# First dense layer of two thirds of the units in seven block products on pairs of units, layers run in turn

## The chip, the cores and the metric

The kernel runs on one core of one Trainium2 chip. The metric is device time in microseconds of one execution, the median of the runs. A TensorE instruction multiplies a stationary block of up to 128x128 (loaded by a weight load of its own) with a moving block of up to 512 columns and adds into a PSUM bank; VectorE (DVE), ScalarE (ACT) and GpSimd (POOL) do elementwise work, and SyncE (SP) issues the transfers.

## The reference, cut to what matters

A chunked linear-attention layer feeds two dense layers. Only the dense part is changed in its arithmetic.

```python
# x (4,8,768,32), a (4,8,768), B and C (4,8,768,16); chunks in the original are 32 long
attn_out = _attn_ref(x, a, B, C)               # decayed C.B scores times x, plus a carried state
x = attn_out.transpose(0, 2, 1, 3).reshape(3072, 256)
def _moe_ref(x, w_in, w_out):                  # layer A; w_in (256,2048), w_out (2048,256)
    h = x @ w_in
    g = h * (1.0 / (1.0 + np.exp(-1.702 * h)))
    return g @ w_out
def _moe2_ref(x, w_in, w_out):                 # layer B, on the result of layer A
    h = x @ w_in
    g = h * np.clip(h + 3.0, 0.0, 6.0) / 6.0
    return g @ w_out
```

## The kernel before

**Tiles.** The 3072 tokens are cut into six blocks of 512 (numbered k), the 2048 hidden columns into sixteen of 128 (m). A unit is one layer, one k and one m: kind A for the first dense layer pair, kind B for the second, so 2 x 6 x 16 = 192 units. A unit first forms a 128x512 bank of hidden values from 256 input features (`l1`, L722), then passes it through its activation, then adds its share to two 128x512 output banks (`l2`, L756). Values and weights are each held as a top half in reduced precision and the rest (`wh`/`wl`, `gh`/`gl`), and three of the four cross products are computed: so `l1` is 2 feature halves x 3 = 6 matmuls of 512 columns and `l2` is 2 output halves x 3 = 6. In this text "first layer" of a unit is `l1`, "second layer" is `l2`; kinds A and B are the two networks.

**Activation.** Kind A: ACT applies the gelu in the bank (L739), casts the top half (L743), DVE or POOL subtracts to get the rest (L753). Kind B: ACT relu into `gg` (L741), DVE clips and multiplies (L748), ACT casts (L743), POOL subtracts (L753).

**Attention.** 32 pieces q (8 chunks of 96 tokens x 4 batches): DVE scans a decay matrix (L460, twice), PE forms scores (L535), DVE or ACT with POOL multiply (L538, L545), PE forms outputs (L556), ACT and DVE split them into the token block's input (L570, L574) and DVE turns the carried state (L583). Chunks 0 to 3 form scores in fp32 from 16 rows, four products at once on the array; chunks 4 to 7 from stacked bf16 parts that pass through DRAM (`stk_store`, `stk_load`).

**Weights** arrive packed in 32 loads and are decoded on the chip (L328 to L362): ACT scales and extracts (L334, L344), DVE joins (L350), ACT casts (L356), POOL subtracts (L362). All 32 stay resident.

**Order.** Nothing runs in loops: the function lists every operation with an engine, an estimated duration and a due time, and `Schedule.run` (L118) sorts them greedily by engine, dependences, free buffers and due times into one straight program. Each engine then runs its list strictly in that order and waits where a value is not there. `order` (L295) gives the units their due times: A0, A1, then B0 and A2 in alternation, B1, then A3, B2, A4, B3, A5, B4, B5. `PIECE` (L70) gives those of the attention pieces: after the first six, five ahead of A1, five ahead of A2, six ahead of A3 and the last ten during A3/B2 and A4/B3. The second layer of a unit is due two units after its first (`LAG`). The pools of buffers are fixed tiles; the hidden banks `h` are two.

Of the kernel before, what the change touches and what calls it, by code (L numbers as in the profile page):

```python
# [61 lines left out]


def YBANK(q):
    if q < 6:
        return f"{'ys'[q % 2]}:y{q}"
    return f"{'ys'[q % 2] if q < 16 else 'y'}:y{q}"


def PIECE(q, lead):  # L70

    if q < 6:
        return 6 + 2.2 * q + 3 * (q > 3)
    if q < 11:
        return lead["A", 1] - 20 + 4 * (q - 6)
    if q < 16:
        return lead["A", 2] - 30 + 5 * (q - 11)
    if q < 22:
        return lead["A", 3] - 42 + 7 * (q - 16)
    k, i = (3, q - 22) if q < 27 else (4, q - 27)  # L80
    return lead["A", k] + 2 + 8 * i
# [831 lines left out]
```

## Time and profile before

| | us |
|---|---|
| median of three runs | 592.24 (591.18 to 592.87) |
| span of the profiled execution (the page gives no other time of it) | 591.0 |
| TensorE matmuls busy, 3260 instructions | 580.1 |
| DVE busy, 453 instructions | 296.8 |
| ACT busy, 596 instructions | 316.3 |
| POOL busy, 165 instructions | 202.3 |

The busy time of PE in the page counts each matmul until its modelled end, so the ends of neighbours overlap; the distance from one to the next is read from the chain or the timeline. A group's mean hides its spread; the source view gives least, median and greatest. The chain of waits is followed back from the last instruction, so an engine with most of the chain sets the end.

### The profile page before, as it was taken

How to read it: one execution, taken by the hardware profiler on the slowest of the kernel's cores; microseconds unless marked ns; L12 is line 12 of the kernel's file. 1: busy time of each engine (PE TensorE's matmuls, PEld its weight loads, DVE VectorE, ACT ScalarE, POOL GpSimd, SP SyncE). 2: the span in 40 equal slices, each digit the busy share in tenths (PEclk: the TensorE clock that was granted, in tenths of full speed). 3: DMA queues.
4: the chain of work that ended last, by engine and by line, in shares of the span. 5: the costliest groups of instructions: out<-in, count | busy, mean ns of one | idle time of the engine just before them, and what ended most of it. 6: DMA issues, size and time to landing. Idle time of an engine off the chain costs nothing.

```text
span 591.0 us, 8575 instructions
## 1 busy us (share of the span) xinstructions
PE 580.1 (98%) x3260; PEld 466.6 (79%) x3260; DVE 296.8 (50%) x453; ACT 316.3 (54%) x596; POOL 202.3 (34%) x165
## 2 busy tenths in 40 slices
PE   8799999999999999999999999999999999999997
PEld 6587777778888887778778888778888888888885
DVE  6899996745434647777533454642322222322221
ACT  2788746677776455454444545334544544444443
POOL 2747200224544445461001662000544000454542
PEclk9899999999999999999999999999999999999999
DMA  8856641522212939566240163200000100000101
GB/s 187 287 141 199 174 116 69 171 76 104 81 62 62 239 93 259 140 165 174 88 145 1 29 151 102 90 24 1 1 1 0 37 1 1 0 2 0 37 0 36
DMA packets 42776, 52.36 MB, mean 89 GB/s; under 512 B 22752, under 2 KB 34384, under 8 KB 42736
## 3 DMA queue, kind: packets, MB, share of 16 engines
q1 hardware_dynamic: 41888, 51.47, 30.7%
q10 hardware_dynamic: 848, 0.35, 0.3%
q8 instruction: 25, 0.41, 0.3%
q14 instruction: 15, 0.12, 0.1%
HBM read 41.21 MB, written 10.60 MB: 88 GB/s over the span
## 4 chain that ended last, share of the span: by engine, by line
PE 95%; DMA 2%; DVE 1%; ACT 1%; issue 0%; SPq 0%; ACTq 0%
PE h L728 45%; PE acc L774 45%; PE y L556 2%; DMA raws<-in_wu 1%; PE s L535 1%; DVE l L460 1%; DMA late<-in_bcz 1%; PE acc L535 1%; PE s L556 1%; PE acc L728 0%; DVE xs L583 0%; DVE xt L574 0%; DVE gl L753 0%; ACT raws L344 0%; ACT gg L787 0%
## 5 line engine op out<-in xcount | busy, mean ns | idle before, releaser
L753 POOL TENSOR_TENSOR gl<-gg,gh 128x512 fp32r<-128x512 f32 x95 | 127.1, 1340 | 274.8 <-ACT gh L743 256.5
L728 PE MATMUL h<-xt,wh 128*128 128x512 f32 x568 | 157.0, 399 | 1.5 <-DVE xt L574 0.8
L748 DVE SCALAR_TENSOR_TENSOR gg<-gg,h 128x512 f32<-128x512 f32 x96 | 65.8, 685 | 135.9 <-ACT gg L741 135.8
L728 PEld LDWEIGHTS h<-xt,wh 128*128 128x128 f32 x568 | 105.6, 190 | 26.0 <-issue 2.1
L753 DVE TENSOR_TENSOR gl<-h,gh 128x512 fp32r<-128x512 f32 x94 | 64.8, 689 | 108.1 <-ACT gh L743 104.9
L774 PE MATMUL acc<-gh,wh 128*128 128x512 f32 x288 | 112.4, 390 | 0.0
L739 ACT ACTIVATE h<-h 128x512 f32<-128x512 f32 x94 | 54.7, 582 | 106.0 <-PE h L728 105.8
L774 PE MATMUL acc<-gh,wl 128*128 128x512 f32 x276 | 109.1, 395 | 0.0
L741 ACT ACTIVATE gg<-h 128x512 f32<-128x512 f32 x96 | 57.4, 598 | 82.4 <-PE h L728 77.3
L774 PE MATMUL acc<-gl,wh 128*128 128x512 f32 x288 | 89.8, 389 | 0.0
L743 ACT CAST gh<-gg 128x512 fp32r<-128x512 f32 x96 | 59.6, 621 | 50.1 <-DVE gg L748 50.1
L728 PE MATMUL h<-xt,wl 128*128 128x512 f32 x272 | 84.8, 393 | 0.0
L460 DVE TENSOR_TENSOR_SCAN l<-l,pat_sb 112x448 f32<-112x448 f32 x52 | 63.3, 1229 | 3.2 <-DMA l<-acl_d 3.1
L774 PEld LDWEIGHTS acc<-gl,wh 128*128 128x128 f32 x288 | 54.1, 188 | 11.5
L774 PEld LDWEIGHTS acc<-gh,wh 128*128 128x128 f32 x288 | 54.1, 188 | 10.9
L774 PEld LDWEIGHTS acc<-gh,wl 128*128 128x128 f32 x276 | 51.8, 188 | 11.9 <-issue 1.2
L728 PEld LDWEIGHTS h<-xt,wl 128*128 128x128 f32 x272 | 51.4, 190 | 11.3 <-issue 0.2
L362 POOL TENSOR_TENSOR wl<-dec,wh 128x512 fp32r<-128x512 f32 x23 | 33.6, 1466 | 71.3 <-ACT wh L356 68.9
L743 ACT CAST gh<-h 128x512 fp32r<-128x512 f32 x94 | 55.2, 587 | 3.6
L728 PE MATMUL h<-xt,w_early 128*128 128x512 f32 x192 | 51.9, 392 | 0.0
L774 PE MATMUL acc<-gh,w_late 128*128 128x512 f32 x108 | 42.4, 392 | 0.0
L728 PEld LDWEIGHTS h<-xt,w_early 128*128 128x128 f32 x192 | 35.6, 188 | 7.6 <-issue 0.3
(96 smaller groups left out, 561.7 us busy)
## 6 DMA issues: line engine op xcount, KB each, us to landing
l<-acl_d SPq DMA_DIRECT2D x26, 392.0 KB, 4.9
raws<-in_wu SPq DMA_DIRECT2D x18, 512.0 KB, 4.8
st<-scr SPq DMA_DIRECT2D x8, 896.0 KB, 6.0
scr<-tsplit SPq DMA_DIRECT2D x32, 168.0 KB, 2.8
raw<-in_wu SPq DMA_DIRECT2D x10, 512.0 KB, 4.0
xs<-in_xs SPq DMA_DIRECT2D x8, 384.0 KB, 5.9
early<-in_wu SPq DMA_DIRECT2D x4, 512.0 KB, 8.4
scr<-tsplit SPq DMA_DIRECT2D x16, 112.0 KB, 2.7
```

Of the source, the lines that this page charges most:

```text
L362: e.tensor_tensor(out=w_lo[p], in0=B_(f"dec:{p}").bitcast(F32), in1=w_hi[p].bitcast(F32), op=ALU.subtract)
L460: nc.vector.tensor_tensor_scan(t, a, m, 0.0, ALU.mult, ALU.add)
L535: nc.tensor.matmul(out=ps[:, k, :], lhsT=l, rhs=r, start=True, stop=True)
L556: nc.tensor.matmul(out=yv[32 * k:32 * k + 32, g, :], lhsT=x[0:E, b, h * D:(h + 1) * D], rhs=B_(f"gm:{q}.{g}")[:, k, :], start=True, stop=True)
L728: nc.tensor.matmul(out=ps, lhsT=w[p][:, 128 * j:128 * j + 128], rhs=x[:, xp, j, a:b], start=not lo and (xp, j) == (1, 0), stop=lo and j == 1)
L739: nc.scalar.activation(ps, ps, AF.Gelu_apprx_sigmoid)
L741: nc.scalar.activation(B_(f"gg:{u}")[:, 0:n], ps, AF.Relu, bias=3.0)
L743: nc.scalar.copy(B_(f"gh:{u}")[:, 0:n], ps if kind == "A" else B_(f"gg:{u}")[:, 0:n])
L748: nc.vector.scalar_tensor_tensor(out=g, in0=g, scalar=6.0, in1=B_(hn(u))[:, 0:n], op0=ALU.min, op1=ALU.mult)
L753: e.tensor_tensor(out=B_(f"gl:{u}")[:, 0:n], in0=g, in1=B_(f"gh:{u}")[:, 0:n].bitcast(F32), op=ALU.subtract)
L774: nc.tensor.matmul(out=acc[d], lhsT=w[p][:, 256 + 128 * d:384 + 128 * d], rhs=g, start=(m == 0 and a == 0 and d not in seen), stop=(m == N ...
```

## The change

**Seven products.** The 64 units of kind A on token blocks 0 to 3 stay as they are. The other 128 (kind A on blocks 4 and 5, kind B on all six) are worked in groups of four: a pair of unit columns m times a pair of token blocks, so 1024 tokens. A group's first layer is a 2x2 by 2x2 product of blocks (two unit columns x two feature halves, two feature halves x two token blocks). Eight block products of 3 matmuls become seven, in Winograd's form: four sums S of weight blocks (`s_comb`) and four of input blocks T1 to T4 (`operands`) are formed and split into halves, and the products go into three banks V, Ra and Rb, with DVE additions (`p_add`) between that carry partial results over through `pu` tiles: u2 = Ra + p1, u3 = Ra + p1, hs = Rb + u3, and two in the bank. A group is called a quad here, and there are 32. Second layers stay 6 matmuls a unit.

**Layers in turn.** The order becomes A0, A1, A2, A3 (units), A4+5 (8 quads), B0+1, B2+3, B4+5 (8 quads each). All 32 attention pieces come ahead of A4+5. All of them form scores in fp32 from 16 rows, two pieces in one go; the bf16 stacks and their DRAM passes are gone. Kind B weights are decoded from A4+5 on, into the sixteen buffers that kind A frees.

**Buffers.** One pool `bx` of 21 tiles of 4 KB holds raw weights, inputs, split inputs, block sums and results by turn; attention's tiles (`ov1` to `ov4`) are reopened for the quads' partial results. Half of the subtractions of A1 to A3 go from DVE to POOL (`GLP`).

```diff
-    for m in range(NM):
-        order += [whole("A", 0, LEAD + m)] * (LEAD + m < NM) + [whole("A", 1, m)]
-    for m in range(NM):
-        order += [whole("B", 0, m), whole("A", 2, m)]
-    order += [whole("B", 1, m) for m in range(NM)]
-    for k in range(3, NK):
-        order += [whole("A", k, m) for m in range(NM)] + [whole("B", k - 1, m) for m in range(NM)]
...
+    units = [("A", k, m) for k in range(STD) for m in range(NM)]
+    sups = [("A", k) for k in range(STD, NB6, 2)] + [("B", k) for k in range(0, NB6, 2)]
...
+PK = (48, 4, 88, 5, 114, 7, 156, 5)
...
+def PIECE(q):
...
     if q < 11:
-        return lead["A", 1] - 20 + 4 * (q - 6)
+        return PK[0] + PK[1] * (q - 6)
...
+    return PK[6] + PK[7] * (q - 22)
...
+GLP = lambda kind, k, m: k > 0 and m % 2 == 0
+TE = lambda kind, v: "DVE" if kind == "A" and v[0] == "T" else "POOL"
+GLQ = lambda kind, j: j == 1 or (kind == "B" and j == 0)
+NBX, NWT, NDEC = 21, 16, 4
...
+        halves("B11", src["B11"], ks[0], ready)
+        sub("T1", src["B12"], src["B11"], "T1", ks[1] - 1.0, [])
+        sub("T2", src["B22"], fs["T1"], "T2", ks[1] - 0.5, [pu["T1"]])
+        halves("T2", fs["T2"], ks[1], [pu["T2"]])
+        halves("T1", fs["T1"], ks[2], [pu["T1"]])
+        halves("B21", src["B21"], ks[3], ready)
+        sub("T3", src["B22"], src["B12"], "T3", ks[4] - 0.5, [])
+        halves("T3", fs["T3"], ks[4], [pu["T3"]])
+        sub("T4", src["B21"], fs["T2"], "T2", ks[5] - 0.5, [pu["T2"], name["T2"], name["T2"] + "l"])
...
+    def product(dst, lhs, n, start):
...
+        hi, lo = lhs()
+        xh, xl = two(n)[:, 0], two(n)[:, 1]
+        for i, (w, x) in enumerate(((hi, xl), (hi, xh), (lo, xh))):
+            nc.tensor.matmul(out=B_(dst), lhsT=w, rhs=x, start=start and i == 0, stop=i == 2, skip_group_check=True)
...
+            pr(t, V, w_of(p0, 0), "B11", w0, True)
+            add("ACT", 0.62, t + 0.7, p_copy, p1, V, r=[V], new=[p1])
+            pr(t + 0.7, Ra, s_of(sw[0], 1), "T2", sw, True)
+            pr(t + 1.4, Rb, s_of(sw[0], 0), "T1", sw, True)
+            add("DVE", 0.71, t + 1.4, p_add, u2, Ra, p1, r=[Ra, p1], new=[u2])
+            pr(t + 3.4, V, w_of(p0, 1), "B21", w0, False)
+            pr(t + 4.1, Ra, s_of(sw[0], 2), "T3", sw, False)
+            add("DVE", 0.71, t + 4.7, p_add, u3, Ra, p1, r=[Ra, p1], new=[u3])
+            add("DVE", 0.71, t + 4.8, p_add, hs, Rb, u3, r=[Rb, u3], new=[hs])
+            pr(t + 6.1, Ra, w_of(p0 + 1, 1), "T4", w1, False)
+            add("DVE", 0.71, t + 6.8, p_add, Ra, Ra, p1, r=[p1], w=[Ra])
+            pr(t + 6.8, Rb, s_of(sw[0], 3), "B22", sw, False)
+            add("DVE", 0.71, t + 7.5, p_add, Rb, Rb, u2, r=[u2], w=[Rb])
```

On PE, where the units of kind A on token block 4 begin (their first one reads `xt_138`), the list before has one first layer and one second layer in turn. `h_151` and `h_152` are the two hidden banks, `acc` the output banks, `w_early` and `w_late` weights.

```order
L774 MATMUL acc_153<-gl_145,w_early 128x512
L774 MATMUL acc_156<-gl_145,w_early 128x512
L728 MATMUL h_152<-xt_137,w_early 128x512 x4
L728 MATMUL h_152<-xt_137,w_late 128x512 x2
L728 MATMUL h_151<-xt_138,wh_72 128x512 x4
L728 MATMUL h_151<-xt_138,wl_96 128x512 x2
L774 MATMUL acc_153<-gh_144,w_late 128x512
L774 MATMUL acc_153<-gh_144,w_early 128x512
L774 MATMUL acc_156<-gh_144,w_late 128x512
L774 MATMUL acc_156<-gh_144,w_early 128x512
```

After, at the same place, the first quad of A4+5 stands; `h_128` is V, `h_127` is Ra, `y_134` and `s_133` are Rb of this and the next quad. V of the quad after it stands ahead of this quad's B22.

```order
L761 MATMUL h_128<-bx_B21A_2246,wh_71 128x512 x2
L761 MATMUL h_128<-bx_B21A_2246,wl_72 128x512
L761 MATMUL h_127<-bx_T3A_2296,bx_SA_939 128x512 x3
L761 MATMUL h_127<-bx_T4A_2302,wh_73 128x512 x2
L761 MATMUL h_127<-bx_T4A_2302,wl_74 128x512
L761 MATMUL h_128<-bx_B11A_2206,wh_75 128x512 x2
L761 MATMUL h_128<-bx_B11A_2206,wl_76 128x512
L761 MATMUL s_133<-bx_B22A_2308,bx_SA_939 128x512 x3
```

The second layers of the last units of A3 now stand between the quad's products, and products T3 and T4 into the same bank stand next to each other.

On DVE, where kind A on token block 5 ends, the list before has one operation for a unit: a subtraction (L753) for kind A, the clip (L748) for kind B, and the split of the finished block (L782).

```order
L753 TENSOR_TENSOR gl2_147<-h0_151,gh0_142 128x512
L753 TENSOR_TENSOR gl0_145<-h1_152,gh1_143 128x512
L748 SCALAR_TENSOR_TENSOR gg1_141<-gg1_141,h0_151 128x512
L748 SCALAR_TENSOR_TENSOR gg0_140<-gg0_140,h1_152 128x512
L782 TENSOR_TENSOR xt2_139<-acc1_154,xt2_139 128x512
L782 TENSOR_TENSOR xt2_139<-acc2_155,xt2_139 128x512
```

After, in the last quads of kind B, DVE has the five additions (L773) of a quad among its four clips (L609) and two subtractions (L615); `ov1` holds u2 and u3, `ov4` hs.

```order
L773 TENSOR_TENSOR ov1_b_2202<-h0_127,ov1_b_2202 128x512
L615 TENSOR_TENSOR ov3_b_2204<-s0_133,ov2_b_2203 128x512
L773 TENSOR_TENSOR ov1_b_2202<-h0_127,ov1_b_2202 128x512
L609 SCALAR_TENSOR_TENSOR gg1_108<-gg1_108,h1_128 128x512
L773 TENSOR_TENSOR ov4_b_2205<-y0_134,ov1_b_2202 128x512
L773 TENSOR_TENSOR h0_127<-h0_127,ov1_b_2202 128x512
L609 SCALAR_TENSOR_TENSOR ov4_b_2205<-gg0_107,ov4_b_2205 128x512
L773 TENSOR_TENSOR y0_134<-y0_134,ov1_b_2202 128x512
L609 SCALAR_TENSOR_TENSOR gg2_109<-gg2_109,h0_127 128x512
L609 SCALAR_TENSOR_TENSOR y0_134<-gg1_108,y0_134 128x512
L615 TENSOR_TENSOR gl1_114<-gg2_109,gh2_112 128x512
```

What moved: eleven operations a quad stand where four clips stood for four units, and each addition into u2, u3 or hs stands between two products on PE.

On PE in those last quads of kind B (`ov_b` as weights is a block sum, `ov_b` ahead of `wl`/`wh` a value's top half or rest):

```order
L761 MATMUL h_128<-bx_B21B_4004,wh_101 128x512 x2
L761 MATMUL h_128<-bx_B21B_4004,wl_102 128x512
L761 MATMUL h_127<-bx_T3B_4112,ov_b 128x512 x3
L625 MATMUL acc_131<-ov_b,wl_96 128x512
L625 MATMUL acc_131<-ov_b,wh_95 128x512
L625 MATMUL acc_130<-ov_b,wl_96 128x512
L625 MATMUL acc_130<-ov_b,wh_95 128x512
L625 MATMUL acc_131<-ov_b,wh_95 128x512
L625 MATMUL acc_130<-ov_b,wh_95 128x512
L761 MATMUL h_127<-bx_T4B_4118,wh_99 128x512 x2
L761 MATMUL h_127<-bx_T4B_4118,wl_100 128x512
```

Between T3 and T4, on the one bank `h_127`, stands one second layer of the quad before.

## Rows read from the trace of the kernel before

**Rows 1.** The page: an engine's busy time (share) xinstructions, and the chain that ended last.

```profile
PE 580.1 (98%) x3260; PEld 466.6 (79%) x3260; DVE 296.8 (50%) x453; ACT 316.3 (54%) x596; POOL 202.3 (34%) x165
...
PE 95%; DMA 2%; DVE 1%; ACT 1%; issue 0%; SPq 0%; ACTq 0%
```

**Rows 2.** Windows: stretch, its length, busy time (xinstructions) of each engine, clock, DMA share, GB/s.

```profile
80.00:90.00 10.00, 9.36 (x41) 7.40 (x41) 9.67 (x14) 5.41 (x10) 0.00 (x0) 1.00 0.64 199
...
90.00:100.00 10.00, 10.00 (x59) 7.90 (x58) 6.27 (x12) 6.45 (x13) 1.30 (x1) 1.00 0.11 43
...
120.00:220.00 100.00, 100.00 (x455) 82.38 (x454) 46.56 (x65) 66.85 (x119) 44.08 (x38) 1.00 0.37 106
...
400.00:500.00 100.00, 100.00 (x447) 82.75 (x442) 27.24 (x40) 45.65 (x79) 20.63 (x16) 1.00 0.02 6
```

**Rows 3.** The chain of waits in order of time: start us, us, step.

```profile
26.46 5.27 PE h L728 x12
...
150.13 1.36 PE h L728 x6
...
151.49 1.36 PE acc L774 x6
...
228.05 2.72 PE h L728 x12
```

**Rows 4.** Groups by line: line engine op xcount | busy us, mean ns | idle before.

```profile
L728 PE MATMUL h<-xt,wh 128*128 128x512 f32 x568 | 157.0, 399 | 1.5 <-DVE xt L574 0.8 <-DVE gl L753 0.6
...
L728 PE MATMUL acc<-xt,wl 128*128 128x512 f32 x4 | 1.2, 390 | 0.0
```

**Rows 5.** Timeline of PE around attention scores: start us, us, engine line op out<-in xcount.

```profile
61.23 0.61 PE L774 MATMUL acc<-gl,wh 128*128 128x512 f32 x2
...
62.76 0.50 PE L774 MATMUL acc<-gh,wl 128*128 128x512 f32 x1
...
239.10 0.61 PE L774 MATMUL acc<-gl,wh 128*128 128x512 f32 x2
...
239.94 1.15 PE L728 MATMUL h<-xt,w_early 128*128 128x512 f32 x4
```

**Rows 6.** Groups by line of DVE, ACT and POOL, columns as in group 4.

```profile
L748 DVE SCALAR_TENSOR_TENSOR gg<-gg,h 128x512 f32<-128x512 f32 x96 | 65.8, 685 | 135.9 <-ACT gg L741 135.8
...
L753 DVE TENSOR_TENSOR gl<-h,gh 128x512 fp32r<-128x512 f32 x94 | 64.8, 689 | 108.1 <-ACT gh L743 104.9 <-POOL tsplit L478 1.8
...
L460 DVE TENSOR_TENSOR_SCAN l<-l,pat_sb 112x448 f32<-112x448 f32 x52 | 63.3, 1229 | 3.2 <-DMA l<-acl_d 3.1
...
L538 DVE TENSOR_TENSOR gm<-acc,l 112x448 f32<-112x448 f32 x26 | 15.7, 613 | 0.0
...
L583 DVE STREAM_TRANSPOSE xs<-st_sb 32x128 f32<-32x128 f32 x56 | 17.1, 305 | 1.5 <-ACT st_sb L560 0.4
...
L743 ACT CAST gh<-h 128x512 fp32r<-128x512 f32 x94 | 55.2, 587 | 3.6
...
L753 POOL TENSOR_TENSOR gl<-gg,gh 128x512 fp32r<-128x512 f32 x95 | 127.1, 1340 | 274.8 <-ACT gh L743 256.5 <-issue 16.3 <-POOL gl L753 0.8
```

**Rows 7.** Timeline of all engines in one unit of kind B, columns as in group 5.

```profile
410.64 0.62 PE L728 MATMUL h<-xt,wl 128*128 128x512 f32 x2
411.29 0.60 ACT L741 ACTIVATE gg<-h 128x512 f32<-128x512 f32 x1 [1.52 <-PE h L728]
411.92 0.69 DVE L748 SCALAR_TENSOR_TENSOR gg<-gg,h 128x512 f32<-128x512 f32 x1 [1.43 <-ACT gg L741]
```

**Rows 8.** The source view of L350: engine op xcount: duration ns min/median/max.

```profile
L350 DVE SCALAR_TENSOR_TENSOR dec<-raws x18: 673/688/1261, 24.9 to 177.9; 128x512 uint32<-128x512 uint32 x18
...
L350 DVE SCALAR_TENSOR_TENSOR dec<-early x4: 675/1439/1804, 28.4 to 39.2; 128x512 uint32<-128x512 uint32 x4
```

**Rows 9.** Timeline at the end of the span, columns as in group 5.

```profile
586.32 0.39 PE L774 MATMUL acc<-gl,w_early 128*128 128x512 f32 x1
...
586.74 1.77 SPq L797 DMA_DIRECT2D out<-gg  x4
```

More of the change, by code (lines that the diff above doesn't have):

```diff
@@ L691, in ssd_moe_kernel @@
+            if k not in taken:
+                taken.add(k)
+                for x in where:
+                    sch.take(x, t + 2)
+            add("ACT", el, t + 2.2, y_out, q, k, a, e, r=[yn, where[0]], w=[f"x{q}.{k}h"])
+            if k < STD:
+                add("DVE", el + 0.02, t + 2.3, y_lo, q, k, a, e, r=[yn, f"x{q}.{k}h", *where], w=[f"x{q}.{k}l"])
         if b % 2 and c + 1 < NC:
             for k in range(4):
-                add("DVE", 0.22, t + 2.4 + 8 * (q == 3), st_turn, c, b // 2, k, after=TURN * (q == 3), r=[f"st_sb{b - 1}", f"st_sb{b}", f"xs:{c + 1}"], w=[f"xs:{c + 1}.{b // 2}.{k}"])
@@ new lines, in l1, with gelu, relu @@
+    def l1(u, low):
+        kind, k, m = units[u]
+        hi, lo = B_(f"wt:{m}")
+        xh, xl = two(f"bx:{k}h"), two(f"bx:{k}l")
+        for w, x, j in ((lo, xh, 0), (lo, xh, 1)) if low else ((hi, xl, 0), (hi, xl, 1), (hi, xh, 0), (hi, xh, 1)):
+            nc.tensor.matmul(out=B_(hn(u)), lhsT=w[:, 128 * j:128 * j + 128], rhs=x[:, j], start=x is xl and j == 0, stop=low and j == 1)
+    def gelu(src, dst):
+        nc.scalar.activation(B_(dst), B_(src), AF.Gelu_apprx_sigmoid)
+    def relu(src, dst):
+        nc.scalar.activation(B_(dst), B_(src), AF.Relu, bias=3.0)
@@ L772, in l2 @@
         seen = set()
         for i, (d, w, g) in enumerate(seq):
-            nc.tensor.matmul(out=acc[d], lhsT=w[p][:, 256 + 128 * d:384 + 128 * d], rhs=g,
-                             start=(m == 0 and a == 0 and d not in seen), stop=(m == NM - 1 and d not in [v[0] for v in seq[i + 1:]]))
+            nc.tensor.matmul(out=B_(acc[d]), lhsT=w[:, 256 + 128 * d:384 + 128 * d], rhs=g,
+                             start=first and d not in seen, stop=last and d not in [v[0] for v in seq[i + 1:]])
@@ new lines, in ssd_moe_kernel, with drain, drains @@
+    parts = {k: [f"x{q}.{k}{v}" for q in block for kk, a, b in block[q] if kk == k for v in ("hl" if k < STD else "h")] for k in range(NB6)}
+    def drain(acc, n, d, e):
+        (nc.scalar.copy if e == "ACT" else nc.vector.tensor_copy)(x_raw(n)[:, d], B_(acc))
+    def drains(k, t):
+        sch.take(f"bx:h{k}", t)
+        for d in range(2):
+            e = ("ACT", "DVE")[d]
+            add(e, 0.62, t, drain, f"acc:A{k}.{d}", f"h{k}", d, e, r=[f"acc:A{k}.{d}", f"bx:h{k}"], w=[f"z{k}.{d}"])
```

665 lines of the change are left out of this document (297 added, 368 removed).

## The prediction, made before the change was run

> **What bounds the kernel now.** I read the page first: PE is busy for 98% of the span and has 95% of the chain that ended last [rows 1]. The windows say where that holds: from 120 to 220 us and from 400 to 500 us PE is busy without a gap while DVE stands at 47% and 27% [rows 2]. In one early stretch, 80 to 90 us, DVE is at 9.67 of 10 us and PE loses 0.64; ten microseconds later DVE is at 6.27 and PE loses nothing [rows 2]. So the kernel is as long as its matmuls, and only a DVE that is nearly full has cost PE anything. The chain gives the price: six matmuls of 512 columns take 1.36 us, in `l1` as in `l2` [rows 3], so 0.2267 us each. The groups by line hold 1152 records of L728 (six groups, the first of 568 and the last of 4 [rows 4]) and as many of L774; 2304 x 0.2267 = 522.3 us. The dense units begin at 26.46 us [rows 3], the last matmul starts at 586.32 and the last output transfers follow [rows 9], so some 38 us of PE between those two are attention pieces and the slow start below.
>
> The profiled span is 591.0 us, the median of the runs 592.24; the sum is made on the span, and 1.2 us are put back at the end.
>
> **The change, part by part.**
>
> *Fewer matmuls.* A quad had 4 units x 12 = 48 matmuls and has 7 x 3 + 4 x 6 = 45. The list for PE agrees: 384 + 672 + 1152 = 2208 against 2304. 32 quads x 3 x 0.2267 = **-21.8 us**, all of it on the path, since PE is the path. The new products have the old shape, 128x128 by 512, and each old matmul already had a weight load of its own, hidden beside the one before it.
>
> *Attention scores of chunks 4 to 7.* These 16 pieces go from bf16 stacks to fp32 rows. A pair of pieces in fp32 takes 62.76 - 61.23 = 1.53 us from the start of two dense matmuls to the next one; less their 0.45 that is 1.08, or 0.54 a piece. A bf16 piece takes 239.94 - 239.10 = 0.84, less 0.45, 0.39 [rows 5]. 16 x 0.15 = 2.4 us more; the first dense matmul after a change of shape is slower by a tenth, and that comes once a pair instead of once a piece, which gives some back. I take **+1.9**, with 0 and 2.4 as ends. The DRAM passes go, but SP was not on the chain.
>
> *The first quad of A4+5.* Its T3 and T4 stand next to each other on one bank and u3 lies between them. After PE's last matmul a reader starts about 0.2 us past the time at which the next could start (410.64 + 0.45 = 411.09, ACT at 411.29), and a DVE operation of this size takes 0.69 [rows 7]: 0.9 us in which PE has nothing it may do, since V of the next quad and B22 stand behind T4 in its list. V of the next quad then wants V's chain of gelu, cast and subtraction (0.59 to 0.69 each [rows 6]) done: some 0.7 more. **+1.6**, ends 0.5 and 3.
>
> *The other 31 quads.* One quad of kind B gives DVE five additions, four clips and two subtractions at 0.69 [rows 6]: 7.6 us of the quad's 45 x 0.2267 = 10.2. ACT has one copy and eight passes at about 0.6, 5.4 us; POOL two subtractions at 1.34 [rows 6], 2.7. DVE is the fullest, at 74%. A quad of kind A has 5 + 3 operations on DVE. The chains that PE waits on are covered: T3 to T4 needs 0.2 + 0.69 = 0.9 and has one second layer, 1.36, between; T3 to B22 needs u3 and hs, 1.6, and has 1.36 + 0.68 = 2.04. No row of before shows these waits, so I bound them by stretches of like DVE load. With DVE at 63% (90 to 100 us) PE lost nothing; at 97% it lost 0.64 in 10 [rows 2], which over 31 x 10.2 = 316 us would be 20. The load here is nearer the first. While kind B's weights are decoded (A4+5 and about half of B0+1), DVE gets another join per 7.5 us and may pass 85%. I take **+1**, with 0 and, at a third of the upper rate, 7.
>
> *Attention drawn forward.* Pieces 6 to 31 now share units 16 to 63. DVE's work there: 52 scans x 1.23, 35 products x 0.62, 48 turns x 0.31, 24 subtractions x 0.69 [rows 6], and about 11 us of smaller ones: 128 us. PE needs 48 x 2.72 = 131 us for the units and for each of 26 pieces (38 - 2.6 of slow start) / 26 = 1.36, 166 us in all. 77% again, because half of the units' subtractions go to POOL. In the list for PE the last piece's output stands behind unit 57 of 64, so seven units, 19 us, are left for forming T1 to T4, about eight DVE operations or 6 us. That cover is what hides `operands`, and without it a piece that is late is paid for in full. POOL has 24 subtractions, 17 products of the pieces and six block sums at about 4.6 us each (two additions, four small ones, a subtraction, scaled from 1.34 for 512 columns): 85 of 166 us. I take **0** beyond the 0.64 that is there already; the upper end is the rate of 80 to 90 us over half of the stretch, 5.
>
> *Start and end.* The lists begin alike: the same loads, the same six pieces, then the units. The twelve matmuls at 26.46 us took 5.27 us where twelve at 228.05 took 2.72 [rows 3]; that slow start is taken over, and if it falls otherwise it gives or takes 2.5. At the end four second layers, 5.4 us, stand between the last product and the one that needs its chain of five operations, 3.3; the transfers after the last matmul stay. **0**.
>
> Here a rule of the Trainium skill speaks against the change. The join has a median of 0.69 us from one set of buffers, but its longest took 1.26, and four from another set reached 1.8 [rows 8]. The Trainium skill's page "SBUF — State Buffer", section "SBUF: two separate sides", says that a DVE operation with two SBUF inputs and a GpSimd operation that reads SBUF exclude each other for a whole instruction; the stretched joins agree. Its result is the second rival.
>
> The sum: 591.0 - 21.8 + 1.9 + 1.6 + 1 = 573.7 us of span, **574.9 us** as a time.
>
> **The rivals.**
>
> *The early stretch overruns.* Scans stretch, since POOL now subtracts and forms block sums beside them; pieces slip past unit 64, and PE stands ahead of A4+5. For: the scan's mean of 1.23 is the largest price on DVE, and 80 to 90 us shows what a full DVE does. Against: 23% of room, and 19 us of cover. Price 5 to 12 us: about 583. Chance 0.12.
>
> *DVE and POOL exclude each other in the quads.* Two of a quad's eleven operations read two SBUF tiles (the clip into hs, one subtraction). If each is stretched by up to 1.1, as the longest join was [rows 8], DVE goes to 9.8 of 10.2: still not the bound, but an addition behind one is late by 1.1 less its spare 0.45. 0.65 in half of 24 quads is 8 us: about 583 too. Chance 0.09. The page named above states this rule.
>
> *PE waits in every quad, and the kernel is slower.* PE's list is strict, Ra is one bank and three products go into it in turn. If u3 and hs each stand behind another DVE operation that has just begun, T3 to B22 takes 0.2 + 4 x 0.69 = 3.0 us against 2.04 of cover: 0.9 a quad. From (21.8 - 4.5) / 32 = 0.54 us a quad the gain is gone; at 0.9 it is 29 us: about 602. For: DVE does have clips between the additions. Against: where the clip stands between u3 and hs, a second layer often stands ahead of B22 too, and DVE idles a quarter of the time. Chance 0.06.
>
> *No gain left.* The last two mixed, within 0.3% of before: 0.03. That the products are not fewer is excluded by the count.
>
> **How the numbers follow.** My forecast has the other 0.70. All lower ends of its terms together give 568, all upper ones 588; they do not hang together, so I take 570 and 581 for it. The 8 in 10 need all of it and part of the first two rivals, which lie just above: 570 to 586. A measurement of this kernel can tell about 0.3%, 1.8 us. Faster by more: 0.70 + 0.12 + 0.09 = 0.91; within: 0.03; slower: 0.06.
>
> **What would show it.** Right: 2208 dense matmuls at 1.36 us per six; between the first quad and the end PE busy without gaps in the windows; one gap of 1 to 2 us between T3 and T4 of the first quad; DVE at about 75% in kind B's quads. The first rival would show as PE idle before the first quad, released by an input's split; the second as long clips and subtractions on DVE beside busy POOL; the third as a wait of `product` on `p_add` in each quad. The forecast is wrong if PE's total wait after 27 us passes 10 us, or if the price of six matmuls is not 1.36.

## The result, and the profile after

The changed kernel takes **584.25 us** (median of four executions, 579.64 to 586.02), the kernel before 592.17 beside it (591.18 to 592.87): a ratio of 0.985, 95% interval 0.981 to 0.990. That is a gain clear of the noise, inside the range of 570 to 586, and less than half of what was forecast: 8 us instead of 17.

The profiled execution is the shortest of the four, span 577.9 us at a mean granted clock of 0.992; the other three have spans of 580.9 to 584.2 and mean clocks of 0.978 to 0.984. The forecast span was 573.7. So there are two questions: why 577.9 and not 573.7, and why most executions are longer still.

The page of the kernel after, its engines and the chain that ended last, as [rows 1]:

```profile
PE 561.2 (97%) x3292; PEld 448.5 (78%) x3292; DVE 433.0 (75%) x614; ACT 343.7 (59%) x652; POOL 311.1 (54%) x283
...
PE 91%; DVE 4%; DMA 2%; ACT 1%; issue 1%; POOL 0%; ACTq 0%; SPq 0%; DVEq 0%
```

PE has 19 us less work, DVE 136 us more and POOL 109 more. Windows (columns as in [rows 2]), the same two long stretches and the places where PE loses time:

```profile
70.00:80.00 10.00, 7.15 (x83) 4.62 (x83) 9.91 (x16) 3.05 (x9) 4.77 (x5) 1.00 0.31 98
...
120.00:220.00 100.00, 100.00 (x857) 75.36 (x856) 72.63 (x96) 49.22 (x108) 51.20 (x41) 1.00 0.27 74
400.00:500.00 100.00, 100.00 (x442) 82.86 (x442) 76.02 (x113) 56.58 (x99) 41.18 (x32) 1.00 0.06 20
240.00:260.00 20.00, 18.68 (x81) 14.83 (x80) 15.35 (x25) 13.52 (x25) 9.72 (x13) 1.00 0.46 153
```

PE runs without a gap where it did before, with DVE at 73 to 76% instead of 27 to 47%. The chain (start, us, step) shows that the price of six matmuls is the one of [rows 3], in the units, in the products (three for 0.68) and in the second layers:

```profile
225.90 1.36 PE h L600 x6
227.26 1.36 PE acc L625 x6
...
240.18 0.68 PE h L761 x3
...
242.22 2.72 PE acc L625 x12
```

**The stall of 70 to 80 us.** PE's waits from 60 to 90 us (engine, line, releaser: us in total, times, longest):

```profile
PE h L600 <- ACT wh L346: 1.7, 1, 1.7
PE s L481 <- DVE ov_a L463: 1.1, 2, 0.7
```

2.85 us, where the kernel before lost 0.64 [rows 2]. The timeline of POOL and DVE there (start, us, what, idle before) shows what delays it; L425 is the scan, L343 the join of a weight, `wl` on POOL the rest of another weight:

```profile
71.84 1.28 POOL L350 TENSOR_TENSOR wl<-dec,wh 128x512 fp32r<-128x512 f32 x1 [4.11 <-ACT wh L346]
...
72.16 1.91 DVE L425 TENSOR_TENSOR_SCAN ov_a<-ov_a,pat_sb 112x448 f32<-112x448 f32 x1
...
75.63 1.09 DVE L425 TENSOR_TENSOR_SCAN ov_a<-ov_a,pat_sb 112x448 f32<-112x448 f32 x1
76.63 0.67 DVE L343 SCALAR_TENSOR_TENSOR dec<-bx_w 128x512 uint32<-128x512 uint32 x1
...
78.01 0.73 PE L600 MATMUL h<-bx_0l,wh 128*128 128x512 f32 x2 [1.74 <-ACT wh L346]
```

The scan that starts beside POOL's subtraction takes 1.91 us and ends 0.95 after POOL does (73.12, 74.07); the next one, with POOL idle, takes 1.09. DVE is full, the last weight's join comes at 76.63, and unit 15 waits for it (through ACT's cast of the joined weight). The 52 scans have a mean of 1498 ns instead of the 1229 of [rows 6].

**The end.** Timeline of PE, DVE and SP's queue, as [rows 9]:

```profile
570.96 0.62 PE L625 MATMUL acc<-ov_b,wh 128*128 128x512 f32 x2
...
573.81 0.69 DVE L780 TENSOR_SCALAR gg<-acc 128x512 f32<-128x512 f32 x1 [2.86 <-DMA out<-gg]
...
570.98 4.36 SPq L783 DMA_DIRECT2D out<-gg  x8
```

Two token blocks now end together: four output banks instead of two, three `gg` buffers for them, so the last scaling waits 2.86 us for a buffer that an earlier transfer still reads, and eight transfers are issued one after another instead of four. From the start of the last matmul (570.96 + 0.23 = 571.19) to the end of the span it is 6.7 us; before it was 591.0 - 586.32 = 4.7.

### The profile page after: what moved, and what is told of

Same layout as the page of the kernel before. It is cut to its first block, busy times and chain, and to the rows that moved or that the text cites. A ratio compares the mean times of both kernels' runs of the same rounds, so it can differ in the third digit from the quotient of the medians.

```text
span 577.9 us, 9020 instructions
## 1 busy us (share of the span) xinstructions
PE 561.2 (97%) x3292; PEld 448.5 (78%) x3292; DVE 433.0 (75%) x614; ACT 343.7 (59%) x652; POOL 311.1 (54%) x283
## 4 chain that ended last, share of the span: by engine, by line
PE 91%; DVE 4%; DMA 2%; ACT 1%; issue 1%; POOL 0%; ACTq 0%; SPq 0%; DVEq 0%
PE acc L625 44%; PE h L761 18%; PE h L600 16%; PE s L761 4%; PE y L761 4%; PE s L460 2%; PE y L481 1%; PE s L481 1%; DMA bx_w<-in_wu 1%; DMA ov_a<-in_bcz 1%; DVE ov_b L773 1%; DVE dec L343 1%; PE h L460 1%; PE acc L600 0%; DVE ov_a L425 0%
## 5 line engine op out<-in xcount | busy, mean ns | idle before, releaser
L615 POOL TENSOR_TENSOR gl<-gg,gh 128x512 fp32r<-128x512 f32 x48 | 66.5, 1386 | 121.0 <-ACT gh L612 78.2
L425 DVE TENSOR_TENSOR_SCAN ov_a<-ov_a,pat_sb 112x448 f32<-112x448 f32 x52 | 76.5, 1498 | 9.0 <-DMA ov_a<-acl_d 8.9
L625 PE MATMUL acc<-ov_b,wh 128*128 128x512 f32 x256 | 78.9, 390 | 0.0
L773 DVE TENSOR_TENSOR ov_b<-h,ov_b 128x512 f32<-128x512 f32 x64 | 44.0, 688 | 43.6 <-PE h L761 43.3
L615 POOL TENSOR_TENSOR ov_b<-ov_b 128x512 fp32r<-128x512 f32 x32 | 42.4, 1324 | 39.3 <-ACT ov_b L612 28.6
L350 POOL TENSOR_TENSOR wl<-dec,wh 128x512 fp32r<-128x512 f32 x32 | 44.3, 1389 | 29.3 <-ACT wh L346 27.6
L603 ACT ACTIVATE h<-h 128x512 f32<-128x512 f32 x46 | 26.8, 583 | 48.9 <-PE h L600 38.9
L625 PEld LDWEIGHTS acc<-ov_b,wh 128*128 128x128 f32 x256 | 48.1, 188 | 10.0
L606 ACT ACTIVATE gg<-h 128x512 f32<-128x512 f32 x48 | 28.7, 598 | 38.8 <-PE h L761 27.6
L615 DVE TENSOR_TENSOR gl<-h,gh 128x512 fp32r<-128x512 f32 x46 | 31.4, 683 | 24.8 <-ACT gh L612 23.8
L625 PE MATMUL acc<-ov_b,wl 128*128 128x512 f32 x128 | 49.9, 390 | 0.0
L470 POOL TENSOR_TENSOR ov_a<-ov_a 112x448 f32<-112x448 f32 x24 | 32.9, 1387 | 27.4 <-ACT ov_a L466 26.8
L603 ACT ACTIVATE gg<-h 128x512 f32<-128x512 f32 x32 | 19.1, 597 | 27.9 <-PE h L600 26.8
L609 DVE SCALAR_TENSOR_TENSOR gg<-gg,h 128x512 f32<-128x512 f32 x48 | 32.5, 678 | 1.4 <-ACT gg L606 1.1
L615 DVE TENSOR_TENSOR gl<-gg,gh 128x512 fp32r<-128x512 f32 x32 | 28.6, 895 | 4.9 <-ACT gh L612 4.7
```

What stands on the lines that cost most here:

```text
L350: e.tensor_tensor(out=lo, in0=B_(f"dec:{p}").bitcast(F32), in1=hi.bitcast(F32), op=ALU.subtract)
L425: nc.vector.tensor_tensor_scan(t, a, pat_sb, 0.0, ALU.mult, ALU.add)
L470: nc.gpsimd.tensor_tensor(out=t, in0=t, in1=B_(f"l:{q}")[:, 4 * g:4 * g + 4], op=ALU.mult)
L603: nc.scalar.activation(B_(dst), B_(src), AF.Gelu_apprx_sigmoid)
L606: nc.scalar.activation(B_(dst), B_(src), AF.Relu, bias=3.0)
L609: nc.vector.scalar_tensor_tensor(out=B_(dst), in0=B_(g), scalar=6.0, in1=B_(h), op0=ALU.min, op1=ALU.mult)
```

## The experiments

All but one of the kernels start from the changed one. One number sorts them: from the first matmul of the first quad to the start of PE's last pair it is 338.4 to 338.6 us in every profiled kernel of the table. What differs between them lies ahead of the quads or behind the last matmul. The columns are start times in us; "last pair" is the last two matmuls. "Filled" means that PE works through matmuls whose result nobody reads (called unread here) where it would wait.

| kernel | unit 0 | unit 16 (first of A1) | first quad | last pair | span |
|---|---|---|---|---|---|
| changed, first profile | 26.8 | 81.6 | 232.5 | 570.96 | 577.9 |
| changed, second profile | 30.2 | 87.5 | 238.4 | 576.87 | 583.8 |
| pause at 12 us filled | 26.6 | 83.8 | 234.7 | 573.23 | 580.1 |
| all early pauses filled | 26.5 | 81.5 | 232.3 | 570.87 | 577.8 |
| all filled, tail on two queues | 27.6 | 81.1 | 232.0 | 570.40 | 575.9 |
| the same, pieces 6 us apart | 27.5 | 81.8 | 232.6 | 571.07 | 576.6 |
| the same, pieces 2 us sooner | 26.8 | 77.7 | 231.0 | 569.41 | 574.9 |

### The same kernel again

> The changed kernel as it is, for more executions. Its executions so far have spans of 577.9, 580.9, 584.0 and 584.2 us, and mean granted clocks of 0.992, 0.984, 0.978 and 0.978: the long ones have more time at the half clock. Theory S (start): the extra half clock lies before 60 us, in continuation of the slow stretch in which the first units run; then executions with a mean near 0.978 show a granted clock under 0.9 in a window between 30 and 50 us and 1.00 behind it. Theory L (later): it follows the stall of 70 to 80 us or the first quad's pause at 240 to 260 us, and a window behind one of these shows it. Both expect spans between 577 and 585 and a median near 584 us.

585.3 us (585.19 to 585.55); all four executions have spans of 583.4 to 583.8 at clocks of 0.977 and 0.978. This profile is one of the long kind, so it can be laid beside the first. Windows, and PE's timeline at two places:

```profile
10.00:15.00 5.00, 3.75 (x49) 2.94 (x48) 4.23 (x7) 2.46 (x6) 1.13 (x1) 0.98 1.05 212
15.00:25.00 10.00, 9.94 (x101) 7.65 (x102) 5.88 (x12) 5.22 (x15) 6.55 (x5) 0.50 1.02 379
25.00:35.00 10.00, 7.54 (x51) 5.14 (x48) 8.53 (x17) 7.51 (x18) 6.69 (x6) 0.50 1.04 325
...
80.00:90.00 10.00, 8.26 (x71) 6.12 (x64) 8.92 (x14) 3.12 (x8) 6.93 (x8) 0.83 0.12 42
```

```profile
13.30 1.03 PE L460 MATMUL h<-ov_a 16*112 16x112 f32 x14 [1.25 <-ACT ov_a L466]
...
30.18 1.22 PE L600 MATMUL h<-bx_0l,wh 128*128 128x512 f32 x2 [1.34 <-DVE bx_0l L498]
```

The granted clock is at its lower level, 1.2 GHz, from 14.8 to 35.3 us; in the first profile it was there from 22.9 to 29.7, in the kernel before from 24.5 to 31.3. What PE did before it fell: a wait of 1.25 us for ACT, which decodes a weight before it copies piece 1's scores. Unit 0 starts 3.4 us later, the first units run at half speed, and there is a second slow stretch of 3.4 us behind the stall: 5.9 us in all by unit 16, 4.4 of them by unit 2 (35.38 against 30.98) and 1.5 behind the stall. Theory S has the place right, though the slow stretch begins ahead of the dense units and not behind them; theory L has a part, the dip at 80 to 90 us.

### The split ahead of the joins

```diff
-        add("DVE", 0.82, k - 1.0, w_join, p, r=[R, f"hi{p}", f"low{p}"], new=[Dn], port=True)
+        add("DVE", 0.82, k - 1.0, w_join, p, r=[R, f"hi{p}", f"low{p}"] + ["x5.0l"] * (0 < p < 4), new=[Dn], port=True)
```

> The joins of the weight groups 1 to 3 are made to wait on DVE for the split of the last input piece of the first units, so DVE does the split first. If the joins ahead of the split make PE's pauses between 22 and 27 us, these shrink by 0.5 to 1.5 us in sum. Theory S (the low clock of the long executions is a longer slow start, set off by these pauses): spans stay at 576 to 578 with mean clocks near 0.99, median about 579 us. Theory L (later): the scatter of the mean clock stays, 0.978 to 0.992, and the median moves by less than 1.5 us.

584.05 us (581.28 to 585.63), clocks from 0.981 to 0.990. PE's wait ahead of unit 0 shrank from 1.33 to 0.85 us and unit 0 starts at 26.18, 0.6 sooner; the scatter stayed. So the pauses of 22 to 27 us don't set off the long slow start, which in the second profile of the changed kernel begins before them. The 0.6 us didn't last either: PE's waits from 60 to 80 us rose from 2.85 to 3.97, a half clock from 80.9 to 84.3 us followed, and unit 16 starts at 84.7.

### Products moved off DVE

```diff
-GMP = lambda q, g: (g == 1 and (q in (0, 1, 2, 3, 4, 6) or q > 15)) or (q, g) in ((3, 0), (4, 0))
+GMP = lambda q, g: (g == 1 and (q in (0, 1, 2, 3, 4, 6, 7, 8, 9, 10) or q > 15)) or (q, g) in ((3, 0), (4, 0))
```

> The second product of the attention pieces 7 to 10 goes from DVE to ACT and POOL, four operations of some 0.62 us. Theory F (PE's waits of 2.85 us between 70 and 80 us come from a full DVE): PE's busy time in that window rises from 7.15 to about 9, span down by 1.5 to 2 us. Rival (the weights' arrival or ACT's pass over them sets the last wait, DVE only looks full): the wait of the unit for the last weight stays at 1.7 us and the span moves by under 0.7. A second rival: POOL beside the scans stretches them more, and the span rises by 1 to 2.

586.81 us (582.22 to 586.94); the profiled one has a clock of 0.977 as the second profile of the changed kernel has, and ends 1.3 us after it; the three long executions have spans of 584.9 to 585.2 where the four of the run before had 583.4 to 583.8. PE's waits from 60 to 90 us are 3.8 us instead of 2.85. The window of 70 to 80 us of this kernel, and its group of scans from 50 to 100 us; under it the same group of the changed kernel:

```profile
70.00:80.00 10.00, 8.05 (x61) 5.59 (x60) 9.88 (x10) 4.42 (x11) 6.54 (x5) 1.00 0.34 98
...
L425 DVE TENSOR_TENSOR_SCAN ov_a<-ov_a,pat_sb 112x448 f32<-112x448 f32 x15 | 27.3, 1841 | 0.0
```

```profile
L425 DVE TENSOR_TENSOR_SCAN ov_a<-ov_a,pat_sb 112x448 f32<-112x448 f32 x17 | 23.7, 1412 | 0.0
```

Four products of 0.62 us left DVE, and DVE is as full as before: with POOL busier the scans rose by 0.43 us each, 6.4 us on fifteen. The second rival holds. The exclusion can be read operation by operation in the changed kernel: DVE's subtractions with one input in PSUM take 658 to 693 ns, all 80 of them; those with both in SBUF 680 to 1806 (32); the clips into `hs`, both inputs in SBUF, have a median of 1006 and reach 1806 (24), and those with one in PSUM 670 to 699 (72). The source view of the scans (least, median and greatest duration in ns) shows both kinds:

```profile
L425 DVE TENSOR_TENSOR_SCAN ov_a<-ov_a,pat_sb x52: 1057/1183/3207, 34.6 to 211.3; 112x448 f32<-112x448 f32 x52
...
L425 DVE TENSOR_TENSOR_SCAN ov_a<-acc,pat_sb x12: 1064/1078/1092, 5.3 to 22.4; 112x448 f32<-112x448 f32 x12
```

Of the 52 with both inputs in SBUF, 24 take 1057 to 1093 ns; each of the other 28, from 1125 ns up, ends 0.94 to 0.97 us after the end of an operation of POOL. The twelve with one input in PSUM keep to about 1.08 us, also beside a POOL operation that had begun before them. The Trainium skill's page "SBUF — State Buffer", section "SBUF: two separate sides", says that the two engines share a port pair as an exclusive lock, held for a whole instruction, and counts a DVE operation with two SBUF inputs among those concerned while GpSimd reads SBUF; the 28 scans, whatever their own start, agree.

### The last bank into the idle buffer

```diff
+    def oname(k, d):
+        return f"{'sf' if (k, d) == (NB6 - 1, 1) else 'gg'}:o{k}.{d}"
+
     def o_scale(k, d, e):
-        v = B_(f"gg:o{k}.{d}"), B_(f"acc:B{k}.{d}")
+        v = B_(oname(k, d)), B_(f"acc:B{k}.{d}")
...
```

> The last of the four output banks is drained into the idle single buffer instead of the three that the other outputs share, so that its scaling does not wait for a transfer of an earlier one. Theory B (buffers): the 2.86 us wait of the last scaling goes, the time behind PE's last matmul falls from 6.5 to about 4.4 us, span down by 2.1. Rival (the transfers themselves end last, one behind the other): the tail stays within 0.5 of 6.5 us.

581.43 us (579.04 to 584.36), clocks from 0.978 to 0.993: the scatter hides an effect of this size in the time, so the trace is read. The scaling's wait is 0.67 instead of 2.86 us, and yet the time from the start of the last pair of matmuls to the end is 6.30 instead of 6.94. SP's queue shows why:

```profile
576.32 2.78 SPq L786 DMA_DIRECT2D out<-gg  x6
579.20 0.85 SPq L786 DMA_DIRECT2D out<-sf  x2
```

Eight issues of 0.43 us follow each other with hardly a gap; the buffer was the smaller part of the wait.

### The last transfers on two queues

With `oname` as above:

```diff
-            add(e, 0.62, t, o_scale, k, d, e, r=[f"acc:B{k}.{d}"], new=[f"gg:o{k}.{d}"])
+            add(e, 0.62, t, o_scale, k, d, e, r=[f"acc:B{k}.{d}"], new=[oname(k, d)])
...
-        nc.sync.dma_start(out=out[c, d, :, a - T * c:b - T * c], in_=B_(f"gg:o{k}.{d}")[:, a - LO[k]:b - LO[k]])
+        (nc.scalar if k == NB6 - 1 else nc.sync).dma_start(out=out[c, d, :, a - T * c:b - T * c], in_=B_(oname(k, d))[:, a - LO[k]:b - LO[k]])
...
```

> The last output bank is drained into the idle single buffer, and the four transfers of the last column block are issued from ACT's queue instead of SP's. With the buffer alone the end came 0.64 us sooner, not 2.1: eight transfers are issued one after another on one queue, 0.43 us each, and the last six stood behind each other. Theory I (the issues are the rest of the tail): the time from the start of PE's last matmul to the end of the span falls from 6.94 (6.30 with the buffer alone) to about 4.9 us. Rival (the transfers share the 16 DMA engines and end no sooner): it stays above 5.9 us.

583.9 us (580.19 to 584.01), clocks from 0.978 to 0.987. The tail is 582.2 - 576.69 = 5.5 us, between the two theories' numbers: 1.4 us sooner than the changed kernel, of which 0.8 are the second queue's.

### The pause at 12 us filled

```diff
+    def dummy(dst):
+        nc.tensor.matmul(out=dst, lhsT=pat_sb[:, 0:E], rhs=pat_sb[:, 0:dst.shape[1]], start=True, stop=True)
+
...
     def s_mm(pieces):
+        for _ in range(5 if pieces == (2,) else 0):
+            dummy(B_(SBANK(2, 0))[0:E, 0:4 * E])
```

> Five bf16 matmuls of 448 columns that nothing reads are put on PE ahead of the scores of piece 2, where it pauses between 12.5 and 13.3 us (0.81 us in the changed kernel's first profile, 1.25 in the second, in which the half clock begins at 14.9 instead of 23 us). Theory P (this pause, early and just ahead of 15 us, decides in which executions the half clock begins there): no execution has a mean clock under 0.985, all spans lie at 577 to 579, median time about 579.5 us. Rival Q (the half clock begins at 15 us by chance, whatever PE does there): the long executions stay, mean clock 0.978 and spans near 584 in half of them or more. Rival R (what fell from 15 to 23 us was the load of fp32 matmuls on the way, not the pause): no change either.

582.22 us, and all four between 581.93 and 582.65, clocks 0.986 and 0.987. Windows (PE's busy time counts the unread matmuls):

```profile
10.00:15.00 5.00, 4.95 (x63) 3.81 (x65) 4.39 (x7) 2.48 (x6) 1.29 (x2) 1.00 1.04 192
15.00:25.00 10.00, 7.90 (x135) 5.16 (x124) 9.14 (x17) 8.68 (x22) 7.48 (x7) 0.81 1.03 382
25.00:35.00 10.00, 8.66 (x35) 6.70 (x28) 6.55 (x14) 7.06 (x16) 5.81 (x4) 0.68 1.04 327
```

The long slow start is gone and the scatter with it, as theory P said; the level of 579.5 was wrong, since the half clock of the later pauses comes now from 21 to 31 us. Of the 28 executions of kernels that run as the changed one for the first 20 us (it and those with the split first, the products moved, the two tails and the pieces 7 us apart), 18 have a mean clock of 0.981 or less; of the 21 in which this pause is filled, none is under 0.986. The kernels with two queues and with the pieces 7 us apart ran beside the first two filled ones: six of their eight executions are long, none of the eight filled ones. The length of the pause alone does not tell which execution falls: PE idled for 0.81 us there in one that didn't and for 0.45 in one that did (the kernel with the idle buffer).

### All early pauses filled

As the kernel above, and in `y_mm`, ahead of half g of piece q, and in `l1`, ahead of unit 0:

```diff
+            for _ in range({(3, 1): 4, (4, 1): 6, (5, 0): 8}.get((q, g), 0)):
+                dummy(B_(YBANK(q))[0:E, 256:512])
...
+        for _ in range(7 if (u, low) == (0, False) else 0):
+            dummy(B_(hn(0))[0:E, 0:4 * E])
```

> As the run before, and 18 shorter ones of 256 columns and 7 of 448 in PE's pauses between 19.5 and 26.8 us (3.6 us in sum). If those pauses set off the half clock of 23 to 29.6 us, it does not come at all: the first six matmuls of the dense units take 1.36 us instead of 2.6 or so, the window of 20 to 30 us shows a clock of 1.00, and the span falls by about 3.3 us below that of the run before (574 us). If PE's idle time is not what it goes by (the DMA's or DVE's activity, or the fp32 shape), the half clock stays at 23 to 30 us, and the dummies cost up to 1 us.

579.87 us (579.14 to 580.16), clocks 0.995 and 0.996; ratio to before 0.979, interval 0.977 to 0.981.

```profile
15.00:25.00 10.00, 9.46 (x147) 6.87 (x140) 9.31 (x17) 8.93 (x22) 7.38 (x7) 1.00 1.03 386
25.00:35.00 10.00, 9.92 (x45) 7.75 (x45) 8.95 (x15) 8.50 (x19) 7.14 (x5) 1.00 1.04 322
...
70.00:80.00 10.00, 8.20 (x75) 5.54 (x76) 9.44 (x17) 2.89 (x10) 6.25 (x7) 0.86 0.27 86
```

The half clock is gone up to 70 us, as expected, and the expected span of 574 is missed by 3.8. The timeline shows where it went: unit 2 starts 1.65 us sooner than in the first profile of the changed kernel (29.33 against 30.98), and unit 16 at nearly the same time (81.48 against 81.60). L609 of this kernel is L600 of the changed one:

```profile
76.37 0.73 PE L609 MATMUL h<-bx_0l,wh 128*128 128x512 f32 x2 [1.74 <-ACT wh L346]
...
81.48 0.62 PE L609 MATMUL h<-bx_1l,wh 128*128 128x512 f32 x2
```

The stall is as long as before, 2.86 us, and ends as much sooner (76.37 against 78.01), so the gain outlasts it. It is lost right behind: the granted clock is at its lower level from 77.15 to 80.56, and unit 16 comes 5.1 us after the stall instead of 3.6. The first profile of the changed kernel has the same stall without that dip; the second one has it. In all, eight of the nine profiles of kernels that keep their waits there show a dip behind them.

### Pieces 7 us apart

```diff
-PK = (48, 4, 88, 5, 114, 7, 156, 5)
+PK = (48, 7, 88, 5, 114, 7, 156, 5)
```

> The due times of the attention pieces 6 to 10 are 7 us apart instead of 4, so that fewer scans stand ahead of the last weights' joins on DVE. Theory O (the order on a DVE that is kept full by scans held up by POOL's weight subtractions: three scans took 1.5 to 1.96 us beside one, 1.08 alone): PE's waits between 60 and 90 us fall from 2.85 us to under 1.2. Rival (the load is the same, the waits only move): the sum of PE's waits between 50 and 110 us stays at 2.4 or more. No effect on the clock's scatter is expected.

585.12 us (583.28 to 587.69), clocks from 0.975 to 0.987. PE loses 3.7 us between 60 and 90 us, 2.5 of them ahead of a piece's output and 0.9 ahead of an input's split, and unit 16 starts at 83.6, a half clock of 81.45 to 88.28 us included: the rival, the waits only moved.

### The same filling in the kernel before

`dummy` as above, put into the kernel before:

```diff
     def s_mm(qs, gs):
+        for _ in range({(2,): 1, (3,): 5}.get(tuple(qs), 0)):
+            dummy(B_(SBANK(2, 0))[0:E, 0:4 * E] if qs[0] == 2 else B_(yname[1])[0:E, 256:512])
...
+            for _ in range({(3, 1): 3, (4, 1): 6, (5, 0): 3}.get((q, g), 0)):
+                dummy(B_(yname[q])[0:E, 256:512])
...
+        for _ in range(4 if u == 0 and not lo else 0):
+            dummy(B_(hn(u))[0:E, 0:4 * E])
```

> The kernel before with the same kind of unread matmuls in its own early pauses (23 in all, 3.1 us of pauses between 13 and 26.5 us). If PE's pauses there set off its half clock of 24.3 to 31.2 us, that goes, the first twelve dense matmuls take 2.72 us instead of 5.27, and the kernel before gains 1.5 to 2.6 us on its median. If the half clock is none of the pauses' doing, it stays as it is, or loses up to 1 us.

593.04 us against 592.40 for the kernel before: ratio 1.001, interval 1.000 to 1.002. No gain, against the expectation. The mean clock rose, from a median of 0.991 to 0.993 and above, and the profiled execution (span 589.6) has a shorter half clock, but not none. Windows of the filled kernel, then of the kernel before:

```profile
24.00:27.00 3.00, 3.00 (x29) 1.74 (x23) 1.93 (x6) 2.04 (x9) 1.77 (x3) 0.50 0.42 116
27.00:35.00 8.00, 7.90 (x35) 6.23 (x34) 6.46 (x11) 7.08 (x13) 4.37 (x4) 0.99 0.92 269
```

```profile
24.00:27.00 3.00, 1.80 (x25) 0.93 (x18) 2.64 (x7) 2.34 (x9) 2.41 (x4) 0.59 0.38 123
27.00:35.00 8.00, 8.00 (x27) 6.36 (x26) 5.85 (x9) 5.19 (x10) 3.87 (x3) 0.73 0.96 279
```

The unread matmuls themselves ran at the half clock and put unit 0 off to 27.11. Eight of the twelve executions have spans of 590.8 to 592.4 and were not profiled; why they are longer stays open. What it settles is that the filling's gain is not a general one: it takes away the long slow start, and that none of 31 executions of the kernel before shows (mean clock 0.985 or more in each; one of them, with a span of 597.7 at a clock of 1.000, is long for a cause that stays open).

### Everything together

The fillings and the idle buffer above, and on top of them:

```diff
+            for _ in range({(3, 1): 4, (4, 1): 6, (5, 0): 8, (9, 0): 4, (9, 1): 6}.get((q, g), 0)):
...
+        for _ in range({0: 7, 15: 8}.get(u, 0) if not low else 0):
...
+    def late(k, d, b):
+        return k == NB6 - 1 and (d == 0 or b < LO[k + 1])
...
+        (nc.scalar if late(k, d, b) else nc.sync).dma_start(out=out[c, d, :, a - T * c:b - T * c], in_=B_(oname(k, d))[:, a - LO[k]:b - LO[k]])
```

> The changed kernel with all fillings (12.5 us, 19.5 to 26.8 us), 10 more unread matmuls around the output of piece 9 and 8 ahead of unit 15, where PE waits for 2.86 us between 68 and 80 us, and the tail with the idle buffer and two queues (three transfers on ACT's, five on SP's). Theory P: the granted clock is 1.00 in every window to the end, the dip of 0.86 behind the stall goes, 0.85 us; the tail gives 1.4 to 1.8. Span near 575.3, median 577.2, all executions within 1 us. Rival: the dip behind the stall stays (it is not the pause that makes it); then the span is 576.2 and the median 578.2.

577.32 us (577.14 to 577.74), ratio 0.975, interval 0.974 to 0.977. The dip behind the stall is gone (clock 1.00 in every window from 26 to 560 us), as in the two kernels below: none of three profiles with this pause filled has it, against eight of nine without. So, as far as three profiles tell, the dip comes only behind the pause, though not behind every one. The span of 575.9 and 575.4 to 575.6 in the others lies where theory P put it. In the profiled execution a half clock of 3.4 us shows at 22 to 25 us, while PE works through unread matmuls: filling does not exclude it.

### Pieces sooner

Two due times of the pieces 6 to 10 on top of all that: `PK = (40, 6, ...` and `PK = (46, 4, ...`, instead of 48 and 4.

> As the run before, with the attention pieces 6 to 10 due at 40, 46, ... 64 us instead of 48, 52, ... 64: DVE is idle for 4 of the 20 us from 30 to 50. If the stall at 68 to 80 us is DVE's whole load up to 81 us (joins, scans, subtractions), work drawn into its idle time ends it sooner: PE's waits of 60 to 90 us fall from 2.86 (some of it filled) to under 1.5, and the median falls by 1 to 2 us. If it is the order alone, or the scans only meet other subtractions of POOL's, the sum stays within 0.7 us of the run before, as with the pieces 7 us apart.

577.81 us (577.58 to 578.38), no gain. PE's idle time from 60 to 80 us is 0.8; in the kernel that it is compared with it is 0.1, since unread matmuls stand in that wait, so idle time can't tell here. From unit 2 to unit 16 it takes 51.4 us instead of 50.6, and unit 16 starts at 81.8.

> As the last but one, with the pieces 6 to 10 due 2 us sooner (46, 50, ... 62 us). The same two theories: half of the effect, 0.5 to 1 us, by DVE's load; within 0.7 us either way by the order alone.

577.07 us (576.73 to 578.49), ratio 0.975, interval 0.973 to 0.977: within 0.7 of the kernel that it is compared with, so DVE's load as the whole cause is not shown. Its profile is the shortest of all, 574.9. Unit 16 starts at 77.7, 3.4 us sooner, and the first quad only 1.0 sooner. Most of the difference was never a gain: PE's list has eight dense matmuls fewer between unit 2 and unit 16 (166 instead of 174) and as many more behind it, 1.8 us, and a wait at 131.8 us for a subtraction of DVE costs another 0.4. Between unit 16 and the first quad PE has no other wait. Both kernels are beaten, the one before by 2.5% and the changed one by about 1% (0.975 against 0.985 of the kernel before).

## Why the prediction was right, and where its terms were off

The direction, the path and the main term held. Two terms were mis-sized (the attention drawn forward and the end), and one, the start, was priced by a single profile. That the range held is in part luck: the median lies above 570 to 581, the range of the forecast itself, and within 586 only because of the room kept for the first two rivals, whose losses of some 8 us did not come; other losses took their place. PE is idle for 4.6 us in all behind 27 us, below the 10 that were to show the forecast wrong. One sum was off without a consequence: all upper ends together, with the 2.5 of the start as in the lower ones, give 590 and not 588.

- **Fewer matmuls, -21.8.** Right: six cost 1.36 us in all three shapes, PE has no gaps in the long windows, and the kernel's gain comes from nothing else.
- **First quad, +1.6, and the other 31, +1.** PE's idle time is 1.3 us in two waits on DVE's addition, and 0.4 in two more.

```profile
245.46 0.84 PE L761 MATMUL h<-bx_T3A,bx_SA 128*128 128x512 f32 x3
247.08 0.73 PE L761 MATMUL h<-bx_T4A,wh 128*128 128x512 f32 x2 [0.78 <-DVE ov_b L773]
...
253.11 0.39 PE L761 MATMUL h<-bx_B21A,wl 128*128 128x512 f32 x1
254.04 0.96 PE L761 MATMUL h<-bx_T3A,bx_SA 128*128 128x512 f32 x3 [0.54 <-DVE ov_b L773]
```

  Idle time is less than what a wait costs, since the view lets the matmul ahead of it last 0.39 us and the next one could start after 0.23. From start to start the first two waits cost 247.08 - 245.46 - 0.68 = 0.94 and 254.04 - 253.11 - 0.23 = 0.70, together the 1.6 of the forecast, and the two others 0.75. The first stands where the text put it, between T3 and T4. The second doesn't: it is T3 of the next quad, which waits for u2, and not V for its chain of gelu, cast and subtraction. The spare of a quad covers stretched clips too: with a median of 1.0 us instead of 0.69 they cost PE next to nothing. The second rival's mechanism is in the trace and its price is not; the third rival is out.
- **Attention drawn forward, 0 beyond 0.64.** Measured 2.85 of idle time, so +2.2; from start to start 3.3 against 0.8, so +2.5, under the upper end of 5. The step that failed is the average: 77% of 166 us was reckoned for units 16 to 63, and the loss lies before unit 16, where DVE has five pieces, the joins and the subtractions to finish. That is the first rival in small, with the scans stretched as it said, but with a weight's join behind them and not an input's split.
- **Scores, +1.9.** A pair takes 155.87 - 154.34 - 0.45 = 1.08 us, as priced. From unit 2 to the last matmul PE's time shrank by 554.75 - 540.21 = 14.5 us. That is 21.8 less for the matmuls and 4.9 more for all waits from start to start (5.7 against 0.8), which leaves 2.3 for the attention pieces, near the upper end of 2.4: the change of shape gave almost nothing back.
- **Start, 0 within 2.5.** In the profiled execution it was -0.6 (unit 2 at 30.98 instead of 31.57). In the long execution that was profiled unit 2 starts at 35.38, +3.8, beyond the range given for it, and the dip behind the stall adds 1.5. The text took the slow start over from one profile of the kernel before; that a pause of a microsecond earlier in the program, at 12 us, could go with one that begins 8 us sooner was not asked. At the median this is about half of the missing gain: the two middle spans, 580.9 and 584.0, lie on average 4.6 us above 577.9, and 577.9 lies 4.2 above 573.7.
- **End, 0.** Measured 6.7 - 4.7 = +2.0. "The transfers after the last matmul stay" is the step that failed: ending two blocks together doubles the transfers behind the last matmul, and the diff says so.

In the profiled execution the terms from start to start give 573.7 + 2.5 (attention) + 2.0 (end) - 0.6 (start) + 0.4 (scores) - 0.2 (quads) = 577.8, against 577.9. The rest, 577.9 to some 584, is in the main the longer half clock at the start, which none of the 21 executions with the pause at 12 us filled shows in its long form. What decides in which execution it comes stays open.

## What to carry to other kernels

Where PE is the path, look at the work that is not the inner loop: what ends together at the end, what must be finished before the first tile that needs it, and what PE does in the microseconds before its clock is wanted; the forecast gain of 3% was halved by these three. Read what a wait costs from start to start; behind a dense matmul the idle time fell 0.16 us short of it here, each time. A profile is one execution: take the start's price from the scatter of several, with their clocks. An operation moved from DVE to POOL may leave DVE as full as before: here four products moved, and the scans, which read two SBUF tiles, grew by more than the products had taken.

## What was not expected of the hardware

The granted clock of a single core differed between executions of one and the same program: half of full speed for 6.8 us in one, for 20.5 us in another, both at the start, and 4.4 us of time with it; behind a 1.74 us pause of PE it fell for 3.4 us in one of these two and not in the other, and that dip cost another 1.5 us. Unread matmuls in a 0.8 to 1.25 us pause removed the long form; those in the later ones removed the short form in two profiles and left 3.4 us of it in three. A scan with two inputs in SBUF ended 0.94 to 0.97 us after POOL's operation in all 28 cases in which it was held up, and none of the 12 with an input in PSUM was. Transfers issued from one queue follow each other at 0.43 us, so by an estimate from that, 4 x 0.43, eight of them put the end off by some 1.7 us more than four; each lands 1.5 to 2.0 us after its issue.
